# Where ScalarE forms g, what an output of the attention begins with, and which steps convert a second couple of weight blocks

## The chip, the cores and the metric

The kernel runs on one core of one Trainium2 chip. Its metric is the time of one execution on the device, in microseconds (us), the median of the runs shown. TensorE (PE) multiplies; its weight loads are a row of their own (PEld). ScalarE (ACT) and VectorE (DVE) do the elementwise work, GpSimd (POOL) a little more of it, and SyncE (SP) starts nearly all transfers. Each engine takes its instructions in the order in which they stand in its own queue.

## The reference

A decayed attention of 2 batches, 8 heads, 768 positions and 64 columns a head is followed by two feed-forward blocks, all in float32. `S` is the state that goes from block to block.

```python
for b in range(nb):
    qb, kb, vb = (q[:, :, sl], k[:, :, sl], v[:, :, sl])
    intra = np.einsum('bhic,bhjc->bhij', qb, kb) * Dmask[None]
    intra = np.einsum('bhij,bhjd->bhid', intra, vb)
    inter = np.einsum('bhid,bhde->bhie', qb * lam_pow[None], kv_state)
    out[:, :, sl] = intra + inter
    kv_state = lam_block * kv_state + np.einsum('bhsd,bhse->bhde', kb_dec, vb)

x = attn_out                      # 1536 tokens x 512
h = x @ w_in                      # 512 x 2048
g = np.maximum(h, 0.0) ** 2
x = g @ w_out                     # 2048 x 512
gate = 1.0 / (1.0 + np.exp(-(x @ w_gate)))
out = (gate * (x @ w_val)) @ w_out2
```

## The kernel before

**Numbers.** A float32 product is made of three products of rounded halves: a block and an operand are each split into a high part, which ScalarE rounds (`whi`, `gh`, `xh`), and a low part, which VectorE subtracts (`wlo`, `gl`, `xl`). The weights arrive as pairs of 32-bit words of double precision (`raw`). ScalarE makes two words of a block (`scale_words`: `j`, then `r`), VectorE shifts and joins them (`join_words`), the joined block is stored to DRAM for later stages, and `couple_split` makes its high and low parts.

**Couples.** The blocks of the first feed-forward block are converted in couples: the output block of step f together with the input block of step f + 2. There are 17 couples. A couple passes three calls: `couple_act` (four ScalarE instructions, and the next two `raw` loads are queued), `couple_dve` (shift and join on VectorE) and `couple_split` (`whi` on ScalarE, `wlo` on VectorE). I number the couples c0 to c16. Three of them are converted ahead of the loop; the two halves of c0 and c1, one block each, are split there too. Step f splits c(f + 2).

**The stage.** The first 512 tokens go through the first feed-forward block while the rest of the attention is still being computed. `step_1(f)` runs for f = 0 to 15. On PE it gives: `stage_a(f)`, 12 matmuls of 128x512 into one PSUM bank; perhaps the attention work of half 2f; `stage_b(f - 1)`, 12 matmuls of `g` and the output block; perhaps the attention work of half 2f + 1. `SLOTS` says which halves have `scores` (16 matmuls into two banks, later masked by VectorE) or `out` (a state update and an output, 96 matmuls and two banks, which ScalarE copies to `xr`). PSUM has eight banks; four hold the sums of `stage_b` throughout.

**Order.** The program's text is the order on every engine; nothing is rearranged (`tc.manual_schedule`). Before the change, ScalarE in one step does the split of a couple, the four word instructions of the next, and then relu, square and `gh` of the step (lines 525, 526, 538). `MORE = (6, 8, 10)` are the steps that split and convert one couple more.

```python
acc = stage_a(1, f)
run(couple_split())
...
couple_act()
...
gs, ops = split_g(elem(1, f, acc))
```

Stores and some loads stand on an agenda of planned times; they enter SP's queue when the planned clock, which counts matmuls, passes their position. SP waits with a store until its block is joined, and everything behind it in the queue waits too.

**Later stages.** Behind this stage stand a Strassen form of the same feed-forward block for the other 1024 tokens, and the same for the second one. The change doesn't touch their code.

Of the kernel before, what the change touches and what calls it, by code (L numbers as in the profile page):

```python
# [14 lines left out]
TB = 512  # L15
WARM = 14
FILL = (10, 4, 6)
MORE = (6, 8, 10)

PAIRS = ((0, 6), (1, 7), (2, 8), (3, 9), (4, 10), (5, 11))  # L20
LEAD = 2
# [17 lines left out]
def retention_moe_kernel(  # L39
# [24 lines left out]
    nc = tc.nc  # L64
# [15 lines left out]
    def bank():  # L80
        return ps.tile([P, 512], F32, tag="p", name="p")
# [25 lines left out]
    qk_t, kv_t = {}, {}  # L107
# [116 lines left out]
    def couple_split():  # L224
        if not whole_t:
            return []
        keys, w = whole_t.pop(0)
        hi, lo = (several(len(keys), name, F32R) for name in ("whi2", "wlo2"))
        nc.scalar.copy(hi, w)
        for n, key in enumerate(keys):  # L230
            split_t[key] = hi[:, n], lo[:, n]
        return [lambda: nc.vector.tensor_tensor(out=lo, in0=w, in1=hi, op=ALU.subtract)]
# [8 lines left out]
    def run(ops):  # L241
        weave(ops, [])
# [82 lines left out]
    sc_t, qd_t, kd_t, at_t, o_t = {}, {}, {}, {}, {}  # L325
    uv_t, tt_t = [], []

    def pv(t):
        return t.rearrange("a (p b) -> a p b", p=4)

    def half(g):
        return slice(64 * g, 64 * g + 64)

    def held_by(tiles, c, g):


        return tiles[c + 1 if c >= SEQ_CH and g == 0 else c]

    def heads(t):
        return t.rearrange("s (h d) -> s h d", h=H)  # L340
# [64 lines left out]
    def att_out(pair):  # L405


        n = pair[0]
        ov = []
        for s, c in enumerate(pair):  # L410
            v = heads(kv_t[c][:, 1, :])
            at = at_t.pop(c)
            o = pv(bank())
            ov.append(o)
            for p in range(4):
                for r in range(2):
                    nc.tensor.matmul(
                        o[half(r), p, :], lhsT=v[:, 2 * p + r, :],
                        rhs=pv(at[:, r ^ s, :])[:, p, :],
                        start=p == 0, stop=n == 0 and p == 3, skip_group_check=True,  # L420
                    )
        if n > 0:
            for p in range(4):
                for s, c in enumerate(pair):
                    for r in range(2):
                        g = r ^ s
                        nc.tensor.matmul(
                            ov[s][half(r), p, :], lhsT=S[half(g), s, p, :],
                            rhs=pv(held_by(qd_t, c, g))[half(g), p, :],
                            start=False, stop=p == 3, skip_group_check=True,  # L430
                        )
            for c in pair:
                qd_t.pop(c)
        o_t[pair] = ov

    def att_state():
# [682 lines left out]
    def attend(half):  # L1119
        load(LOADS.get(half, ""))  # L1120
        what, k = SLOTS.get(half, (None, 0))
        if what == "scores":
            att_scores(k)
            passed(SCORES)

            def after():
                run(att_mask(k))
                att_keys(k)
                query(k if k < SEQ_CH else k + 1)
                qk_t.pop(k)  # L1130

            return after
        if what == "out":
            pair = PAIRS[k]
            if k < SEQ_CH - 1:
                decayed()
            att_uv(pair)
            att_out(pair)
            for c in pair:
                kv_t.pop(c)  # L1140
            passed(REST)

            def after():
                att_state()
                att_x(pair)

            return after
        return lambda: None

    def step_1(f):  # L1150

        acc = stage_a(1, f)
        run(couple_split())
        while rest:
            rest.pop()()
        attend(2 * f)()
        couple_act()
        if prev:
            stage_b(*prev.pop())
        last = attend(2 * f + 1)  # L1160
        gs, ops = split_g(elem(1, f, acc))
        run(ops)
        run(couple_dve())
        last()
        if f in MORE:
            run(couple_split())
            couple_act()
            run(couple_dve())
        if f + 1 in MORE:
            load_w(2)  # L1170
        prev.append((1, f, gs))
# [25 lines left out]
    with tc.manual_schedule():  # L1197
        load("q6", nc.scalar)
        decays()
        load("q0 q7 v0 v6 w q1 q8 v1 v7 w w w q2 q9")  # L1200
        warm_up(WARM)
        new_xr()
        first, second = PAIRS[:LEAD]
        for c in first:
            att_scores(c)
        warm_up(FILL[0])
        for c in first:
            att_keys(c)
        run([op for c in first for op in att_mask(c)])
        att_uv(first)  # L1210
        for c in (7, 1, 8):
            query(c)
        couple_act()
        for c in second:
            att_scores(c)
        att_out(first)
        att_state()
        x = att_x(first)
        run([op for c in second for op in att_mask(c)])
        run(couple_dve())  # L1220
        warm_up(FILL[1])
        run(x)
        lo = couple_split()
        couple_act()
        run(lo)
        att_out(second)
        run(couple_dve())
        x = att_x(second)
        run(x)
        lo = couple_split()  # L1230
        run(lo)
        couple_act()
        load("v2 v8")
        for c in second:
            att_keys(c)
        decayed()
        att_uv(second)
        run(couple_dve())
        rest.append(att_state)
        for c in (0, 6, 1, 7):  # L1240
            qk_t.pop(c)
        for c in (0, 6, 1, 7):
            kv_t.pop(c)
        clock[0] = 0.0
        flush()


        keys = [(1, i, 0) for i in range(NF1 // 2)]
        prepare_a(keys[0], T1)
        at(T1 - 20.0, lambda: load_a((1, 1, 0)))  # L1250
        combine_x(1, [T1 + d for d in (-25, -22, -19.5, -17, -14, -10, -7, -4, -1, 2, 4)])
        for f in range(NF1):
            step_1(f)
        n_out = 24
        for k in range(3):
            at(T2 - 14.0 + k, lambda: load_w(1))
        for k in range(n_out):
            convert(T2 + 1.0 + k * (T3 - T2 - 4.0) / n_out)
        for f in range(NF1):
            prepare_out(1, f, T2 + 24 * MM * f)  # L1260
        uses = [use for i in range(NF1 // 2) for use in pair_in_1(i)]
        strassen(keys, uses, (None, lambda: close(1)))
        xc.clear()
        new_xr()
        for f in range(2):
            at(T3 - 24.0 + f, lambda f=f: load_units(2, f))
        at(T3 - 14.0, lambda: run(split_w(2, 0)))
        pair_out(1)


        for f in range(2, NF2):
            at(T3 + (36 * (f - 1) - 12) * MM - 8.0, lambda f=f: load_units(2, f))
        for k in range(3 * NF2 - n_out):
            convert(T3 + 2.0 + 3.6 * k)
        for i in range(NF2 // 2):
            sum_out_w(i, T4 - 64.0 + 9.0 * i)
        keys = [(2, i, u) for i in range(NF2 // 2) for u in range(2)]
        prepare_a(keys[0], T4)
        at(T4 - 28.0, lambda: combine_a((2, 0, 1)))
        at(T4 - 20.0, lambda: load_a((2, 0, 1)))  # L1280
        combine_x(2, [T4 - 46.0 + 3.5 * k for k in range(11)])
        for f in range(NF2):
            step_2(f)
        T6 = T5 + 6 * STEP
        by_unit_through_dram(1, T5 - 14.0, T5 - 7.0)
        through_dram(2, T5 - 4.0, T5 + 1.5)
        through_dram(3, T5 + 1.0, T5 + 6.5)
        through_dram(4, T5 + 6.0, T5 + 11.5)
        for n, load, pos in (
            (0, -21.0, -13.0), (1, -12.0, -1.5), (2, -6.0, 4.0),  # L1290
            (3, 1.0, 8.8), (4, 6.0, 13.5), (5, 11.0, 18.3),
        ):
            prepare_w(0, n, n, T5 + load, T5 + pos)
        for n, i, load, pos in (
            (0, 5, -12.5, -5.0), (1, 4, -7.5, -1.0), (2, 3, -3.0, 3.5),
            (3, 0, 1.0, 8.0), (4, 2, 6.0, 12.5), (5, 1, 10.0, 15.5),
        ):
            prepare_w(1, n, i, T6 + load, T6 + pos)
        by_unit_through_dram(2, T6 - 7.0, T6 + 5.0)
        by_unit_through_dram(1, T6, T6 + 10.2)  # L1300
        uses = [use for i in range(NF2 // 2) for use in pair_in_2(i)]
        strassen(keys, uses, (None, lambda: close(2)))
        blocks_out()
        flush()
        assert not agenda and not to_conv and not ready
# [62 lines left out]
```

## Time and profile before

| | us |
|---|---|
| median of 3 runs | 606.05 (604.37 to 606.98) |
| the profiled execution, its own time | 606.55 |
| its span, first to last instruction | 604.8 |
| PE busy in the span | 581.0 (96%) |
| DVE busy | 442.5 (73%) |
| ACT busy | 348.3 (58%) |
| POOL busy | 53.2 (9%) |

The page shows busy time by engine, the span in slices, the queues, the chain that ended last and the costliest groups. Busy PE time includes matmuls at the lower of its two clocks (1.2 against 2.4 GHz), which the windows show as a granted clock of 0.50. A row of the timeline gives the start, the length, engine, line, operation, what is written from what, the number of instructions merged, and in brackets how long the engine had been idle and what ended that.

### The profile page before, as it was taken

The page shows a single profiled execution, that of the slowest core. Times are in us where ns is not written, and L with a number is a line of the kernel's source. Part 1 is how long each engine was busy: PE and PEld are TensorE (multiplying, and loading weights), DVE is VectorE, ACT ScalarE, POOL GpSimd, SP SyncE. Part 2 cuts the span into 40 slices and gives each one's busy share as a digit, 9 for nine tenths or more (in the row PEclk, how much of TensorE's full clock was granted, in tenths as well). Part 3 has the DMA queues.
Part 4 walks back from the last instruction along what each step waited for, and adds up shares of the span by engine and source line. Part 5 has one row for each costly group of instructions (what it writes and reads, how often), then busy time and mean ns, then how long its engine had stood idle before and what let it go on. Part 6 is the DMA issues. An engine that isn't in the chain of part 4 may idle for free.

```text
span 604.8 us, 8511 instructions
## 1 busy us (share of the span) xinstructions
PE 581.0 (96%) x3024; PEld 470.7 (78%) x3024; DVE 442.5 (73%) x632; ACT 348.3 (58%) x548; POOL 53.2 (9%) x51
## 2 busy tenths in 40 slices
PE   8879999888999999999999999999999999999996
PEld 4658777667888888888888888888887888878884
DVE  7765765758688886677674778885578878689964
ACT  3655677576756556666664865534636554475460
POOL 4244240000000000000000000021011101000000
PEclk9979999797999999999999999999999999999999
DMA  8997798532143539999997679994446688488671
GB/s 315 407 411 261 282 310 296 191 106 70 34 157 124 207 104 359 353 412 410 409 407 272 250 253 359 358 303 98 142 111 168 192 249 222 149 321 300 217 279 69
DMA packets 69226, 150.25 MB, mean 248 GB/s; under 512 B 6976, under 2 KB 15168, under 8 KB 69184
## 3 DMA queue, kind: packets, MB, share of 16 engines
q1 hardware_dynamic: 65312, 144.86, 66.8%
q0 software_dynamic: 3360, 3.93, 4.4%
q10 hardware_dynamic: 512, 0.92, 0.5%
q8 instruction: 23, 0.38, 0.3%
q14 instruction: 19, 0.16, 0.1%
HBM read 105.91 MB, written 42.21 MB: 245 GB/s over the span
## 4 chain that ended last, share of the span: by engine, by line
PE 63%; DVE 6%; ACT 5%; DMA 4%; issue 3%; SPq 1%; DVEq 0%; ACTq 0%
PE p L703 27%; PE p L1094 14%; PE p L494 12%; PE p L508 8%; DMA gr<-gs 4%; DVE gq L890 2%; PE p L1023 1%; DVE wq L980 1%; DVE c L717 1%; DVE gs L838 1%; ACT j L154 1%; ACT r L159 1%; DVE j L170 1%; ACT ah L676 1%; DVE al L682 1%
## 5 line engine op out<-in xcount | busy, mean ns | idle before, releaser
L703 PE MATMUL p<-xch,ah 128*128 128x512 f32 x280 | 109.9, 392 | 1.0 <-ACT s L712 0.5
L703 PE MATMUL p<-xcl,ah 128*128 128x512 f32 x280 | 109.0, 389 | 0.0
L703 PE MATMUL p<-xch,al 128*128 128x512 f32 x280 | 109.0, 389 | 0.0
L703 PEld LDWEIGHTS p<-xch,ah 128*128 128x128 f32 x280 | 52.5, 188 | 15.0 <-ACT s L712 3.2
L703 PEld LDWEIGHTS p<-xch,al 128*128 128x128 f32 x280 | 52.6, 188 | 11.0
L712 ACT COPY s<-p 128x512 f32<-128x512 f32 x60 | 35.2, 588 | 45.0 <-PE p L703 44.9
L703 PEld LDWEIGHTS p<-xcl,ah 128*128 128x128 f32 x280 | 52.6, 188 | 10.6
L1023 PE MATMUL p<-gq,wq 128*128 128x512 f32 x252 | 58.3, 391 | 1.6 <-DVE wq L980 1.1
L1023 PEld LDWEIGHTS p<-gq,wq 128*128 128x128 f32 x252 | 47.0, 188 | 12.7 <-DVE wq L980 2.2
L717 DVE TENSOR_TENSOR c<-p,s 128x512 f32<-128x512 f32 x60 | 41.2, 687 | 20.0 <-PE p L703 19.1
L154 ACT ACTIVATE j<-raw 128x512 f32<-128x512 f32 x68 | 45.3, 666 | 9.0 <-DMA raw<-in_w 6.6
L170 DVE CUSTOM_DVE_ANT_0 j<-j,r 128x1024 uint16<-128x1024 uint16 (+1 forms) x53 | 46.4, 875 | 4.9 <-DVE j L165 0.5
L1094 PE MATMUL p<-g2h,whi 128*128 128x512 f32 x128 | 49.8, 389 | 0.0
L1094 PE MATMUL p<-g2l,whi 128*128 128x512 f32 x128 | 49.8, 389 | 0.0
L1094 PE MATMUL p<-g2h,wlo 128*128 128x512 f32 x128 | 49.8, 389 | 0.0
L540 DVE TENSOR_TENSOR gl<-g,gh 128x512 fp32r<-128x512 f32 x28 | 19.8, 708 | 40.5 <-ACT gh L538 40.5
L159 ACT ACTIVATE r<-raw 128x512 int32<-128x512 uint32 x68 | 45.0, 661 | 2.1 <-DMA w<-j 1.9
L494 PE MATMUL p<-xh,whi 128*128 128x512 f32 x160 | 43.7, 395 | 0.1
L508 PE MATMUL p<-gh,whi 128*128 128x512 f32 x112 | 35.5, 434 | 8.1 <-ACT gh L538 8.1
L494 PE MATMUL p<-xh,wlo 128*128 128x512 f32 x160 | 42.9, 390 | 0.0
L494 PE MATMUL p<-xl,whi 128*128 128x512 f32 x160 | 42.8, 389 | 0.0
L651 POOL DMA_DIRECT2D as<-w x6 | 5.6, 926 | 382.0 <-DMA u<-w 306.4
(126 smaller groups left out, 1044.8 us busy)
## 6 DMA issues: line engine op xcount, KB each, us to landing
raw<-in_w SPq DMA_DIRECT2D x68, 512.0 KB, 7.4
w<-j SPq DMA_DIRECT2D x68, 256.0 KB, 6.6
u<-w SPq DMA_DIRECT2D x52, 256.0 KB, 5.4
a<-w SPq DMA_DIRECT2D x20, 512.0 KB, 4.0
g<-g SPq DMA_DIRECT2D x32, 256.0 KB, 4.3
g<-g SPq DMA_DIRECT2D x16, 512.0 KB, 7.7
kv<-in_kv SPq DMA_DIRECT2D x12, 512.0 KB, 7.0
gr<-gs SPq DMA_DIRECT2D x24, 256.0 KB, 6.0
```

The costliest lines, as they stand in the source:

```text
L154: nc.scalar.activation(j, t[:, :, 1].bitcast(F32), AF.Prelu, scale=2.0**-80 if flip else 2.0**-112, alpha=2.0**-32 if flip else 2.0**32,)
L159: nc.scalar.activation(r, low, AF.Copy, scale=2.0**-29)
L170: nc.vector.tensor_tensor(out=j, in0=j, in1=r, op=ALU.add)
L494: nc.tensor.matmul(acc, lhsT=a[:, kk * P : (kk + 1) * P], rhs=b[:, kk, :], start=i == 0, stop=i == 11,)
L508: nc.tensor.matmul(acc[e], lhsT=a[:, e * P : (e + 1) * P], rhs=b, start=first and i == 0, stop=last and i == 2,)
L540: lambda: nc.vector.tensor_tensor(out=gl, in0=src, in1=gh, op=ALU.subtract)
L703: nc.tensor.matmul(acc, lhsT=w[:, col, kk * P : (kk + 1) * P], rhs=x[:, kk, :], start=start and i == 0, stop=stop and i == 5, skip_group_c ...
L712: nc.scalar.copy(s, acc)
L717: nc.vector.tensor_tensor(out=c, in0=acc, in1=s, op=ALU.add)
L890: nc.vector.tensor_tensor(out=block_of(gq[i][1], n), in0=raw.pop(n), in1=block_of(gq[i][0], n), op=ALU.subtract,)
L1023: nc.tensor.matmul(acc[k], lhsT=a[:, wn], rhs=block_of(b, gn), start=first and n == 0, stop=last and n == 3 * len(group) - 1,)
L1094: nc.tensor.matmul(acc[e, t], lhsT=a[:, e * P : (e + 1) * P], rhs=b[:, t, :], start=first and i == 0, stop=last and i == 2,)
```

## The change

In `step_1` the order of the text changes: after `stage_a` come relu, square and `gh`, then the split of a couple, and the word instructions after that. Masks of a half 2f stand ahead of `gl`. In `att_out` the 32 matmuls with the state `S` come first, and open the sums that the 64 with `at` then finish. Ahead of the loop the state of the first pair, its decay and the decayed keys of the second pair stand earlier. Steps 4, 5, 7 and 8, not 6, 8 and 10, convert a second couple, and they no longer split a second one.

```diff
-MORE = (6, 8, 10)
+MORE = (4, 5, 7, 8)
@@ att_out
+        ov = [pv(bank()) for _ in pair]
         if n > 0:
             ...
-                            start=False, stop=p == 3, skip_group_check=True,
+                            start=p == 0, stop=False, skip_group_check=True,
+        for s, c in enumerate(pair):
+            ...
+                        start=n == 0 and p == 0, stop=p == 3, skip_group_check=True,
@@ step_1
         acc = stage_a(1, f)
-        run(couple_split())
         while rest:
             rest.pop()()
-        attend(2 * f)()
-        couple_act()
+        h = 2 * f
+        masks = SLOTS.get(h, ("", 0))[0] == "scores"
+        after = attend(h)
+        gs, ops = split_g(elem(1, f, acc))
+        if masks:
+            after()
+        run(ops)
+        if not masks:
+            after()
+        run(couple_split())
         if prev:
             stage_b(*prev.pop())
-        last = attend(2 * f + 1)
-        gs, ops = split_g(elem(1, f, acc))
-        run(ops)
+        after = attend(h + 1)
+        couple_act()
+        after()
         run(couple_dve())
-        last()
         if f in MORE:
-            run(couple_split())
             couple_act()
             run(couple_dve())
@@ ahead of the loop
         att_uv(first)
+        att_state()
         for c in (7, 1, 8):
             query(c)
+        decayed()
         ...
         att_out(first)
-        att_state()
         ...
+        for c in second:
+            att_keys(c)
         att_out(second)
         ...
-        for c in second:
-            att_keys(c)
-        decayed()
         att_uv(second)
```

ScalarE's queue at steps 0 and 1 before the change; `whi_392` is the split of c2, the next four rows are the words of c3, the three after them belong to step 0:

```order
L229 CAST whi_392<-j_340 128x1024
L154 ACTIVATE j_397<-raw 128x512
L159 ACTIVATE r_398<-raw 128x512
L154 ACTIVATE j_397<-raw 128x512
L159 ACTIVATE r_398<-raw 128x512
L525 ACTIVATE r<-p 128x512
L526 ACTIVATE g<-r 128x512
L538 CAST gh<-g 128x512
```

The same place after the change (its line numbers are two lower here):

```order
L523 ACTIVATE r<-p 128x512
L524 ACTIVATE g<-r 128x512
L536 CAST gh<-g 128x512
L229 CAST whi_401<-j_346 128x1024
L154 ACTIVATE j_405<-raw 128x512
L159 ACTIVATE r_406<-raw 128x512
L154 ACTIVATE j_405<-raw 128x512
L159 ACTIVATE r_406<-raw 128x512
```

The three instructions of g moved from behind five others to ahead of them.

ScalarE's queue before, around step 11: the words of c16, the first split of x (`xch`), the split of c16, then g:

```order
L154 ACTIVATE j_1335<-raw 128x512
L159 ACTIVATE r_1336<-raw 128x512
L154 ACTIVATE j_1335<-raw 128x512
L159 ACTIVATE r_1336<-raw 128x512
L586 CAST xch<-xr 128x1024
L229 CAST whi_1359<-j_1335 128x1024
L525 ACTIVATE r<-p 128x512
L526 ACTIVATE g<-r 128x512
L538 CAST gh<-g 128x512
```

After the change, around the same `xch`:

```order
L229 CAST whi_1317<-j_1046 128x1024
L584 CAST xch<-xr 128x1024
L523 ACTIVATE r<-p 128x512
L524 ACTIVATE g<-r 128x512
L536 CAST gh<-g 128x512
L229 CAST whi_1359<-j_1054 128x1024
L584 CAST xch<-t 128x1024
```

All words are converted by then, c16's in step 9, and one split a step follows g of its step.

## Rows read from the trace of the kernel before

**Rows 1.** Windows: three stretches; engines' busy us, granted clock, DMA share, GB/s.
```profile
0.00:22.30 22.30, 19.38 (x252) 13.08 (x252) 18.08 (x27) 8.95 (x15) 10.90 (x16) 1.00 0.90 344
22.30:159.90 137.60, 123.17 (x853) 98.51 (x854) 89.14 (x98) 90.43 (x141) 24.19 (x17) 0.91 0.67 239
159.90:604.80 444.90, 438.44 (x1921) 359.13 (x1919) 335.27 (x509) 248.87 (x394) 18.11 (x18) 1.00 0.73 247
```

**Rows 2.** Timeline: PE rows of the stage that follow an idle stretch.
```profile
31.73 2.07 PE L508 MATMUL p<-gh,whi 128*128 128x512 f32 x4 [3.65 <-ACT gh L538]
...
44.45 1.91 PE L347 MATMUL p<-qk 64*128 64x128 f32 x14 [2.45 <-DVE at L373]
...
67.43 1.16 PE L347 MATMUL p<-qk 64*128 64x128 f32 x14 [0.58 <-DVE at L373]
...
109.64 2.07 PE L347 MATMUL p<-qk 64*128 64x128 f32 x14 [2.68 <-DVE at L373]
...
138.09 2.08 PE L508 MATMUL p<-gh,whi 128*128 128x512 f32 x4 [4.49 <-ACT gh L538]
```

**Rows 3.** Windows: the four stretches at the lower clock, the first row and the sum.
```profile
31.00:37.80 6.80, 6.07 (x18) 4.46 (x20) 4.95 (x4) 2.34 (x5) 6.80 (x5) 0.50 1.04 411
...
sum 23.30, PE 21.34 PEld 16.87 DVE 18.55 ACT 14.74 POOL 7.48; mean PE 5.33 PEld 4.22 DVE 4.64 ACT 3.69 POOL 1.87
```

**Rows 4.** Timeline, PE: matmuls at the lower clock, then at the higher.
```profile
33.60 1.91 PE L508 MATMUL p<-gh,wlo 128*128 128x512 f32 x4
...
35.30 1.91 PE L508 MATMUL p<-gl,whi 128*128 128x512 f32 x4
...
155.34 1.07 PE L494 MATMUL p<-xh,wlo 128*128 128x512 f32 x4
...
156.24 1.07 PE L494 MATMUL p<-xl,whi 128*128 128x512 f32 x4
```

**Rows 5.** Timeline, steps 0 and 1: PE, VectorE and ScalarE.
```profile
24.29 1.07 PE L494 MATMUL p<-xl,whi 128*128 128x512 f32 x4
...
25.34 1.23 DVE L170 CUSTOM_DVE_ANT_0 j<-j,r 128x2048 uint16<-128x2048 uint16 x1
...
26.60 1.05 ACT L229 CAST whi<-j 128x1024 fp32r<-128x1024 f32 x1 [1.55 <-DVE j L170]
27.01 1.07 PE L494 MATMUL p<-xl,whi 128*128 128x512 f32 x4
27.55 0.67 ACT L154 ACTIVATE j<-raw 128x512 f32<-128x512 f32 x1
...
29.79 0.57 ACT L525 ACTIVATE r<-p 128x512 f32<-128x512 f32 x1
...
31.05 0.62 ACT L538 CAST gh<-g 128x512 fp32r<-128x512 f32 x1
```

**Rows 6.** Timeline, VectorE at steps 4 and 5.
```profile
61.88 0.69 DVE L540 TENSOR_TENSOR gl<-g,gh 128x512 fp32r<-128x512 f32 x1 [4.27 <-ACT gh L538]
62.49 0.69 DVE L165 TENSOR_SCALAR j<-j 128x1024 int32<-128x1024 int32 x1
63.21 1.23 DVE L170 CUSTOM_DVE_ANT_0 j<-j,r 128x2048 uint16<-128x2048 uint16 x1
65.55 1.22 DVE L232 TENSOR_TENSOR wlo<-j,whi 128x1024 fp32r<-128x1024 f32 x1 [1.12 <-ACT whi L229]
66.69 1.28 DVE L373 TENSOR_TENSOR at<-p,D 128x512 f32<-128x512 f32 x2
69.60 0.69 DVE L540 TENSOR_TENSOR gl<-g,gh 128x512 fp32r<-128x512 f32 x1 [1.63 <-ACT gh L538]
```

**Rows 7.** Timeline: VectorE and POOL at the same time, step 1.
```profile
31.75 1.78 POOL L355 TENSOR_TENSOR qd<-qk,L 128x512 f32<-128x512 f32 x1
...
32.31 1.77 DVE L165 TENSOR_SCALAR j<-j 128x1024 int32<-128x1024 int32 x1
...
34.12 1.95 DVE L170 CUSTOM_DVE_ANT_0 j<-j,r 128x2048 uint16<-128x2048 uint16 x1
```

**Rows 8.** Timeline, POOL: the first rows that wait for transfers.
```profile
30.75 1.04 POOL L363 TENSOR_TENSOR kd<-kv,W 128x512 f32<-128x512 f32 x1 [10.78 <-DMA kv<-in_kv]
...
47.32 1.04 POOL L363 TENSOR_TENSOR kd<-kv,W 128x512 f32<-128x512 f32 x1 [9.11 <-DMA kv<-in_kv]
```

More of the change, by code (lines that the diff above doesn't have):

```diff
@@ L408, in att_out @@
         n = pair[0]
[L409 to L421, printed above, removed]
+        ov = [pv(bank()) for _ in pair]
         if n > 0:
@@ L433, in att_out @@
                 qd_t.pop(c)
+        for s, c in enumerate(pair):
+            v = heads(kv_t[c][:, 1, :])
+            at = at_t.pop(c)
+            for p in range(4):
+                for r in range(2):
+                    nc.tensor.matmul(
+                        ov[s][half(r), p, :], lhsT=v[:, 2 * p + r, :],
+                        rhs=pv(at[:, r ^ s, :])[:, p, :],
+                        start=n == 0 and p == 0, stop=p == 3, skip_group_check=True,
+                    )
         o_t[pair] = ov
```

## The prediction

> **What bounds the kernel now.** I read the windows first, cut where the first feed-forward product starts (22.3 us) and where the Strassen blocks start (159.9 us) [rows 1]. Behind 159.9 PE is busy 438.44 of 444.90 us at the full clock: little is to be had there, and the change doesn't touch it. Between the two cuts PE is busy 123.17 of 137.60 us, so it idles 14.4 us, and the granted clock is 0.91 on average. The whole change lies in this stretch and just ahead of it.
>
> The idle time is five pieces that the timeline shows, 13.85 us together [rows 2]. Two end with `gh` (3.65 and 4.49 us), three with the masks (0.58, 2.45 and 2.68 us). Behind each of the four longer ones the granted clock is 0.50; behind the one of 0.58 us it isn't. The windows over those four stretches hold 21.34 us of PE busy time [rows 3]. Four matmuls take 1.70 us from start to start there and 0.90 us at the full clock [rows 4], so this work would have taken 21.34 x 0.90 / 1.70 = 11.3 us: 10.0 us are lost to the clock. PE's work in the stage is thus 123.2 - 10.0 = 113.2 us, 7.1 us a step over 16 steps. Taking all of both away would shorten the kernel by 24.4 us.
>
> Then the cause. At step 0 PE's first input product ends at 24.29 + 1.07 = 25.36 us, but relu starts at 29.79: it stood behind `whi`, which waited for VectorE's join, and four word instructions [rows 5]. In the steps after, the distance from one `gl` to the next is 69.60 - 61.88 = 7.72 us [rows 6]. That is a ring and not PE's pace: ScalarE does split, words, relu, square and `gh`; only then VectorE has `gl`, and behind it shift and join; only then ScalarE may split the next couple. `gl` idled 4.27 us for `gh` there.
>
> **g ahead of the conversions.** No instruction is added or removed, only order. Relu, square and `gh` take 31.05 + 0.62 - 29.79 = 1.88 us [rows 5]. They need only the step's own input product, whose weights were split a step earlier, so they fill the time in which the join runs. The ring that is left is split 0.95 (27.55 - 26.60), words 2.24 (29.79 - 27.55), then shift and join, of which 0.69 + 1.23 less some 0.4 of overlap remain: 4.7 us a step [rows 5, 6]. ScalarE's whole work is 0.95 + 2.24 + 1.88 = 5.1 us, VectorE's 0.69 + 0.69 + 1.23 + 1.22 = 3.8, and 1.28 more for masks [rows 6]. All are below PE's 7.1, so PE becomes the bound.
>
> What is queued behind the new wait: relu now stands at the head of ScalarE's queue until `stage_a` ends, with the split and the words behind it. VectorE waits for those, and PE two steps later. The cover is that lead.
>
> *Step by step at the start.* Relu can start at 25.4, `gh` ends at 27.3, `whi` of c2 (joined at 25.34 + 1.23 = 26.57) at 28.35, and `stage_a(1)` ends at 27.01 + 1.07 = 28.1 [rows 5]. So `stage_b(0)` starts at 28.35, not 31.73, and waits once more for `wlo`: 1.22 behind `whi` against four matmuls in 0.90. I charge 0.6 us. Then c3: words to 30.6, shift and join, split, the four words of c4, and only then relu of step 2. The build gives the second of the two score matmul banks of step 2 the bank which that relu reads, so PE stops there. Shift and join take 1.9 us undisturbed or 3.7 beside POOL (1.77 + 1.95, [rows 7]); relu then ends 0.6 or 2.2 us behind `stage_a(2)`. POOL's keys start at 30.75, when their transfer lands [rows 8], so some disturbance is likely: I take 1.4. The score matmuls of step 7 have the same bank order; there ScalarE is free in time, and the wait is relu alone, 0.6 (0.57 in [rows 5]). In the other steps I find splits and joins ahead of their matmul by 1 us or more. Sum of the new waits: 2.6 us, between 0 and 4.
>
> The piece at 138.09 us goes because relu there stood behind a split of x and behind `whi` of c16, which waited for its join; now g stands first. The two long waits for masks go with the ring: VectorE did `gl`, shift and join ahead of the masks, and all came late.
>
> **State ahead of intra.** The same 32 and 64 matmuls in another order: 0 us. They need `qd` and `S` 2 us earlier and `at` 1 us later; POOL makes `qd` a step ahead. If POOL is late, the price is its longest row here, 1.78 us, for each of four outputs; I keep this in the range.
>
> **Ahead of the loop.** The copy of the state now stands ahead of c0's words and delays them; the four masks ahead of their join on VectorE are the cover. 0 us.
>
> **Other steps for the second couples.** 17 couples as before. An extra couple costs ScalarE 2.24 and VectorE 1.9 us in its step, so ScalarE has 7.3 us in steps 4, 5, 7 and 8, VectorE up to 8.4 in step 4 with two masks. Steps 5 and 8 hold outputs and are longer on PE. The splits left over move to steps 11 to 14: 0.95 and 1.22 us in steps with no words. No term. The loads change place: two `raw` of c6 now stand behind four stores and a query. In this stretch the transfers run at 411 GB/s with a share of 1.04 [rows 3]. Behind the load that lands at 30.75 [rows 8] stand 4.2 MB up to c6, 10.2 us, so c6 lands at 41. ScalarE wants it in step 3 behind g and the split: step 1's product ends at 28.1, step 3's two steps of 7.1 us later at 42.3, and 1.88 + 0.95 make it 45. Cover 4 us.
>
> **The sum.** 606.55 (the profiled execution) - 14.4 (idle) - 10.0 (clock) + 2.6 (new waits) = 584.75. The median of the runs is 0.5 us below this execution: 584.2 us. The stage's first Strassen block would start at 159.9 - 21.8 = 138.
>
> **The rivals.** *POOL in VectorE's way.* For it: [rows 7], a couple's shift and join 1.8 us longer. With masks the ring then has 4.7 + 1.8 + 1.3 = 7.8 us against 7.1: 0.7 in each of eight score steps, 5.6 us, and one fall of the clock at step 2 if the wait reaches the 2.45 us that was enough in [rows 2]; a stretch of 6.8 us at the lower clock costs 6.8 x 0.47 = 3.2. That gives 590 to 593. Against it: PE is two steps ahead of the ring, and out steps are longer.
>
> The Trainium skill, "SBUF — State Buffer", section "Who interferes with whom", speaks for this rival: VectorE and GpSimd share a port pair under an exclusive lock, and the later one fully blocks. The rows agree: the shift came 0.56 us into a POOL row of 1.78, and 1.22 left plus 0.69 of its own is 1.91 against 1.77 measured. By that rule alone two POOL rows a score step, at the mean of 24.19 / 17 = 1.42 us [rows 1], would stand in the ring whole: 4.7 + 1.3 + 2.8 = 8.8 against 7.1, 1.7 in eight steps, and the sum would be near 598.
>
> *Transfers.* If c6 to c8 land late by what is now ahead of c6's loads (1.57 MB at 411 GB/s, 3.8 us), steps 3 to 5 lose up to 11.4 us: 596. Against it: the 4 us of cover.
>
> *Given back later.* The next stage needs blocks from DRAM and the split x; if it were bound by something that doesn't move, the time stays near 606. Against it: PE idles only 6.5 us behind 159.9 [rows 1].
>
> *Slower: the clock.* Small waits at the scores take the place of few long ones. If each of the eight score slots pulled the clock down, 8 x 3.2 = 25.6 us would eat the 21.8: 610. It decides between a gap of 0.58 us, after which the clock stayed, and 2.45, after which it fell [rows 2]; my waits are 0.6 to 1.4, in three places and not eight.
>
> **How the numbers follow.** Forecast 584.2: 0.58. POOL's contention, 588 to 593: 0.26. Transfers, 593 to 602: 0.07. Given back, within 3 us of 606: 0.05. Slower: 0.04. A measurement of this kernel can tell some 0.5%, 3 us. Faster 0.91, same 0.05, slower 0.04. The range runs from 580 (no new wait at all gives 581.6, and attention work may close up a little) to 593, the far end of the contention.
>
> **What would show it.** Right: PE's idle time between the cuts falls from 14.4 to under 4 us, the granted clock there is 1.00 or nearly, relu starts within 0.1 us of the end of `stage_a` in nearly all steps, and the first Strassen block starts near 138 us. The waits that remain are PE for relu or `whi` in steps 1, 2 and 7. Contention: VectorE's shifts near 1.8 us in score steps, and PE waiting for `wlo` or masks. Transfers: ScalarE's words waiting for `raw` loads. The forecast is wrong if a stretch at 0.50 remains in the middle of the stage, or if idle time appears behind the first Strassen block.

## The result, and the profile after

| | before | after |
|---|---|---|
| median of 4 runs, us | 606.51 (604.37 to 607.35) | 586.52 (585.15 to 588.53) |
| the profiled execution, its own time | 606.55 | 585.15 |
| its span | 604.8 | 583.4 |
| PE busy in the span | 581.0 (96%) | 570.9 (98%) |

The ratio of the times is 0.968, with an interval of 0.964 to 0.972: 3.2% faster. The forecast was 584.2 us; 586.5 lies in its range. The two profiled executions differ by 21.4 us where the sum said 21.8. Of the 2.3 us between forecast and median, 0.4 is the sum's; 1.4 is the distance of the profiled execution of after, the fastest of its four runs, from their median; and 0.5 is that of before, which lay above its own and which I carried over.

The windows of the changed kernel, cut where the first feed-forward product starts and where the Strassen blocks start (columns as in [rows 1]):

```profile
0.00:22.10 22.10, 19.29 (x252) 13.12 (x253) 17.10 (x28) 9.19 (x15) 11.19 (x16) 1.00 0.90 343
22.10:137.50 115.40, 113.20 (x856) 90.36 (x853) 88.96 (x96) 87.70 (x138) 28.30 (x17) 1.00 0.76 286
137.50:583.40 445.90, 438.45 (x1921) 359.22 (x1919) 337.69 (x511) 251.34 (x397) 18.11 (x18) 1.00 0.73 246
```

Against [rows 1] the stage takes 115.4 us and not 137.6. PE's busy time there fell from 123.17 to 113.20, its idle time from 14.4 to 2.2, and the granted clock is 1.00 throughout: none of the four stretches at 0.50 is left. ScalarE and VectorE are nearly as busy as before (87.7 and 89.0 us against 90.4 and 89.1), POOL some 4 us more. The part behind the stage is 1.0 us longer (445.9 against 444.9).

PE's rows in the timeline that follow an idle stretch, from the first feed-forward product to 150 us:

```profile
28.09 1.19 PE L506 MATMUL p<-gh,whi 128*128 128x512 f32 x4 [0.24 <-ACT whi L229]
...
36.19 1.16 PE L347 MATMUL p<-qk 64*128 64x128 f32 x14 [0.27 <-ACT r L523]
...
77.94 1.16 PE L347 MATMUL p<-qk 64*128 64x128 f32 x14 [0.27 <-ACT r L523]
...
128.84 1.20 PE L506 MATMUL p<-gh,whi 128*128 128x512 f32 x4 [1.28 <-ACT whi L229]
...
147.98 0.50 PE L701 MATMUL p<-xch,ah 128*128 128x512 f32 x1 [1.71 <-ACT s L710]
```

These answer to [rows 2]. The waits of 3.65 and 4.49 us for `gh` and those of 0.58, 2.45 and 2.68 for the masks are gone. Three small ones stand where the prediction put them (steps 1, 2 and 7). The last two, 1.28 us in step 14 and 1.71 behind the stage, it did not have.

ScalarE's timeline in steps 0 to 2 shows the new order at work:

```profile
25.17 0.60 ACT L523 ACTIVATE r<-p 128x512 f32<-128x512 f32 x1 [0.52 <-PE p L492]
...
26.46 0.62 ACT L536 CAST gh<-g 128x512 fp32r<-128x512 f32 x1
26.99 1.04 ACT L229 CAST whi<-j 128x1024 fp32r<-128x1024 f32 x1
...
35.54 0.60 ACT L523 ACTIVATE r<-p 128x512 f32<-128x512 f32 x1 [0.27 <-PE p L492]
```

At step 0 relu waits for PE now: it starts at 25.17 us, where it started at 29.79 in [rows 5].

### The profile page after: what moved, and what is told of

It reads as the page before. It is cut to its first block, busy times and chain, and to the rows that moved or that the text cites. A ratio compares the mean times of both kernels' runs of the same rounds, so it can differ in the third digit from the quotient of the medians.

```text
span 583.4 us, 8536 instructions
## 1 busy us (share of the span) xinstructions
PE 570.9 (98%) x3024; PEld 462.7 (79%) x3024; DVE 443.8 (76%) x632; ACT 348.2 (60%) x548; POOL 57.6 (10%) x51
## 4 chain that ended last, share of the span: by engine, by line
PE 82%; ACT 6%; DVE 5%; DMA 3%; issue 2%; DVEq 0%; ACTq 0%
PE p L701 27%; PE p L492 17%; PE p L1092 15%; PE p L506 10%; PE p L1021 8%; DMA qk<-in_qk 2%; PE p L427 2%; PE p L347 2%; DVE gq L888 1%; DVE c L715 1%; PE p L415 1%; ACT xch L584 1%; ACT whi L229 1%; DMA gr<-gs 1%; ACT r L523 1%
## 5 line engine op out<-in xcount | busy, mean ns | idle before, releaser
L715 DVE TENSOR_TENSOR c<-p,s 128x512 f32<-128x512 f32 x60 | 41.2, 687 | 20.6 <-PE p L701 19.7
L538 DVE TENSOR_TENSOR gl<-g,gh 128x512 fp32r<-128x512 f32 x28 | 21.1, 753 | 21.1 <-ACT gh L536 21.1
L492 PEld LDWEIGHTS p<-xh,wlo 128*128 128x128 f32 x160 | 30.0, 188 | 6.3
```

The source lines that it names most:

```text
L492: nc.tensor.matmul(acc, lhsT=a[:, kk * P : (kk + 1) * P], rhs=b[:, kk, :], start=i == 0, stop=i == 11,)
L538: lambda: nc.vector.tensor_tensor(out=gl, in0=src, in1=gh, op=ALU.subtract)
L715: nc.vector.tensor_tensor(out=c, in0=acc, in1=s, op=ALU.add)
```

## The experiments

All times are medians; each ratio is against runs of the kernel before that were taken beside it. The kernels ran on more than one chip, so the ratios are the better comparison.

| kernel | us | ratio (95% interval) |
|---|---|---|
| after | 586.5 | 0.968 (0.964 to 0.972) |
| before with the new order in `step_1` alone | 587.2 | 0.969 (0.966 to 0.971) |
| after, second couples in steps 6, 8, 10 | 586.8 | 0.966 (0.964 to 0.969) |
| after, outputs begin with intra | 586.2 | 0.966 (0.963 to 0.968) |
| after with the old order | 617.6 | 1.018 (1.014 to 1.021) |
| after with the old order and steps 6, 8, 10 | 607.4 | 1.001 (1.000 to 1.003) |
| after, split ahead of g | 592.1 | 0.977 (0.973 to 0.981) |
| after, words ahead of g | 591.7 | 0.976 (0.973 to 0.979) |
| after, POOL's products made twice | 595.2 | 0.981 (0.978 to 0.983) |
| before, dummy matmuls in two gaps | 605.9 | 0.999 (0.997 to 1.001) |
| after, two more splits in step 10 | 583.6 | 0.963 (0.960 to 0.966) |
| after, second half of x 2.7 us earlier | **582.1** | 0.960 (0.958 to 0.963) |
| after, both | 582.6 | 0.961 (0.959 to 0.964) |

### Which of the four edits earns the time

The order in `step_1` alone, put into the kernel before (second couples in 6, 8, 10; the old outputs; the old order ahead of the loop):

```diff
         acc = stage_a(1, f)
-        run(couple_split())
...
-        couple_act()
...
+        gs, ops = split_g(elem(1, f, acc))
...
+        run(couple_split())
         if prev:
             stage_b(*prev.pop())
...
-        gs, ops = split_g(elem(1, f, acc))
...
+        couple_act()
...
         if f in MORE:
-            run(couple_split())
```

> The kernel before with the new text of step_1 alone: second couples stay at steps 6, 8, 10 (without their second split), outputs begin with intra, the work ahead of the loop is as before. Theory (the order of g and the conversions earns nearly all of it): 586 to 590 us, PE idle in the stage under 5 us, no stretch at clock 0.50. Rival (the placement of the second couples, or the state first, earns it): 597 us or more.

587.2 us, 0.969. From 22.1 us to its first Strassen block at 138.86 PE idles 3.5 us, at a granted clock of 1.00. The order alone gives the whole gain that can be measured; what the three other edits add is within the measurement (0.969 against 0.968). Taken out of the changed kernel one at a time, two of them show the same:

```diff
-MORE = (4, 5, 7, 8)
+MORE = (6, 8, 10)
```

> The changed kernel with the second couples back at steps 6, 8 and 10. As predicted, placement carries no term: 585 to 588.5 us. Rival (words left for step 10 collide with the first splits of x, or the earlier loads were what kept ScalarE fed): 590 us or more.

586.8 us.

```diff
 att_out
+        (the 64 products with at first)
         (the 32 products with S)
-        (the 64 products with at)
```

> The changed kernel with outputs that begin with intra again. As predicted 0 us: 585 to 588 us. Rival (the masks end so late that the order with at first stops PE in the four outputs): 589 us or more.

586.2 us. Both terms were rightly set to nothing. The order ahead of the loop was not taken out by itself, and neither were two parts of the new `step_1`: the masks ahead of `gl` and the second split that is no longer done. What each of these does alone is not shown.

Then the reverse: the changed kernel with the old order.

```diff
         acc = stage_a(1, f)
+        run(couple_split())
...
+        couple_act()
...
         gs, ops = split_g(elem(1, f, acc))
...
-        run(couple_split())
...
-        couple_act()
         if f in MORE:
+            run(couple_split())
```

> The changed kernel with the old text of step_1: everything else stays changed, so second couples are split and converted at steps 4, 5, 7, 8. Theory: 603 to 609 us, the distance from gl to gl is still 7.7 us in plain steps. Rival: 597 us or less.

A miss: 617.6 us, 1.8% slower than before, where 603 to 609 was expected. The timeline of that kernel between 73 and 103 us, first ScalarE, then PE:

```profile
73.37 1.06 ACT L229 CAST whi<-j 128x1024 fp32r<-128x1024 f32 x1 [2.62 <-DVE j L170]
...
78.37 1.04 ACT L229 CAST whi<-j 128x1024 fp32r<-128x1024 f32 x1 [1.67 <-DVE j L170]
...
81.56 0.57 ACT L523 ACTIVATE r<-p 128x512 f32<-128x512 f32 x1
```

```profile
82.19 2.08 PE L492 MATMUL p<-xh,whi 128*128 128x512 f32 x4 [2.74 <-ACT r L523]
...
96.84 0.79 PE L347 MATMUL p<-qk 64*128 64x128 f32 x2 [3.50 <-ACT r L523]
...
102.28 2.07 PE L347 MATMUL p<-qk 64*128 64x128 f32 x14 [4.65 <-DVE at L373]
```

Between the `gh` at 70.13 and the next relu stand these two splits, each of which waits for its join, and eight word instructions. Relu comes at 81.56 and PE, which needs its bank, stops for 2.74 us, and again for 3.50 one step later. The distance from `gl` to `gl` in plain steps is 7.71 and 7.72 us, as expected. To see whether the second couples do this or the two other edits, the old steps were put back into the same kernel:

```diff
-MORE = (4, 5, 7, 8)
+MORE = (6, 8, 10)
```

> The changed kernel with the old order in step_1 and the old steps (6, 8, 10) of the second couples; so the kernel before with only the outputs that begin with the state and the new order ahead of the loop. Theory (with the old order a second couple lengthens the ring of its step, 4.1 us of ScalarE more ahead of relu, and steps 7 and 8 in a row leave PE no time to recover; the other two edits carry nothing, as with the new order): 604 to 608, and the waits of 2.7, 3.5 and 4.7 us at 82 to 102 us that the kernel with the old order and steps 4, 5, 7, 8 showed are gone. Rival (the state first or the order ahead of the loop does the harm with the old order, since relu's late bank now holds a state product up): 612 to 618, and the waits at 82 to 102 us stay.

607.4 us, ratio 1.001, and of the waits at 82 to 102 us only one of 1.78 us for masks is left: the second couples did it, and the outputs and the order ahead of the loop together carry nothing with the old order either. (A second couple is one split and four words, 0.95 + 2.24 = 3.2 us of ScalarE by [rows 5], not the 4.1 of the expectation.) So the steps of the second couples cost 10 us with the old order, and with the new one no more than can be measured (586.8 against 586.5).

### What has to stand ahead of what

The split ahead of g, the words still last:

```diff
         acc = stage_a(1, f)
...
+        whole = couple_split()
...
-        run(couple_split())
+        run(whole)
```

> The changed kernel with the split of the couple (whi) ahead of g on ScalarE; the words stay last. The ring is then split 0.95, g 1.88, words 2.24, join 1.5: 6.6 us a step, 8.4 with a join beside POOL, against PE's 7.1. Theory: 588 to 595 us, some of the gain goes in the score steps. Rival 1 (only the four word instructions ahead of g did harm): 586 to 587. Rival 2 (anything that waits ahead of g takes the gain back): 600 or more.

592.1 us, in the range of the theory; where it is lost, though, is not where the theory had it, as shown below. The words ahead of g, the split behind it:

```diff
         acc = stage_a(1, f)
...
+        couple_act()
...
         after = attend(h + 1)
-        couple_act()
```

> The changed kernel with the four word instructions ahead of g on ScalarE and the split behind it. The words wait for nothing but their load; the join runs while ScalarE does g and the split. Theory of the ring (what cost the time was that g and gl stood between words and join and the next split): 585 to 589 us. Rival (g must be first, 2.24 us later g costs PE in each of the ten steps with words): 595 us or more.

591.7 us, between the two. The trace says why. PE and ScalarE at the start of the stage, then the windows:

```profile
31.10 1.31 PE L506 MATMUL p<-gh,whi 128*128 128x512 f32 x4 [3.04 <-ACT whi L229]
33.16 2.07 PE L506 MATMUL p<-gh,wlo 128*128 128x512 f32 x4 [0.75 <-DVE wlo L232]
```

```profile
25.94 0.68 ACT L154 ACTIVATE j<-raw 128x512 f32<-128x512 f32 x1 [1.09 <-DMA raw<-in_w]
...
28.21 0.58 ACT L523 ACTIVATE r<-p 128x512 f32<-128x512 f32 x1
```

```profile
31.00:40.00 9.00, 8.15 (x33) 5.89 (x34) 8.89 (x5) 7.21 (x13) 8.36 (x5) 0.62 1.03 408
40.00:141.50 101.50, 100.15 (x793) 80.60 (x792) 74.14 (x84) 71.98 (x112) 18.94 (x12) 1.00 0.69 254
```

At step 0 the words wait 1.09 us for a load, relu comes 3.0 us later than in the changed kernel, and PE loses the difference and the clock (0.62) up to 40 us. From there on PE idles only 1.35 us in 101.5, of which 1.29 is the wait of step 14 that the changed kernel has too. So in the running stage the words may stand on either side of g, as the ring argues; at its start, where PE has no lead yet, they may not. The split ahead of g loses in the same place and more: PE waits 1.26 us for `gh`, 0.66 for `wlo` and then 2.55 for the masks. Steps 3 to 13 lose nothing more, the score steps among them; from step 14 on it is not 4.8 us behind the changed kernel (126.61 against 121.86 at `stage_b` of step 13) but 7.2 (144.67 against 137.50 at the first Strassen block).

```profile
29.13 1.20 PE L506 MATMUL p<-gh,whi 128*128 128x512 f32 x4 [1.26 <-ACT gh L536]
...
30.99 1.20 PE L506 MATMUL p<-gh,wlo 128*128 128x512 f32 x4 [0.66 <-DVE wlo L232]
...
40.10 1.78 PE L347 MATMUL p<-qk 64*128 64x128 f32 x14 [2.55 <-DVE at L373]
```

### The clock by itself

The prediction took 14.4 us of idle time and 10.0 us of lower clock as two terms. Here the kernel before gets 14 and 18 matmuls of a constant tile in bfloat16, whose result nobody reads (3.2 and 4.1 us of PE), ahead of `stage_b` in steps 1 and 11:

```diff
+IDLE = {1: 14, 11: 18}
...
         couple_act()
+        if f in IDLE:
+            warm_up(IDLE[f])
         if prev:
             stage_b(*prev.pop())
```

> The kernel before with matmuls of no use to the result put into two of its idle stretches: 14 ahead of the output product of step 0 (gap of 3.65 us) and 18 ahead of that of step 10 (gap of 4.49 us). They leave the gaps as long as they are and show what the lower clock behind them costs. The sum of the prediction (10.0 us for four stretches, each worth about 3.2): 600 us. If the first stretch lies beside ScalarE's ring and only the second is on PE's path: 603. If neither: 606. If the clock stays low all the same, the granted clock shows it.

605.9 us, ratio 0.999: no gain that can be told from none. Windows over three of the four stretches of [rows 3] in this kernel (its line numbers are one higher):

```profile
31.00:37.80 6.80, 6.21 (x38) 4.91 (x38) 5.01 (x4) 2.32 (x4) 6.80 (x5) 1.00 1.04 408
44.00:48.20 4.20, 3.79 (x18) 3.27 (x19) 3.40 (x5) 4.17 (x7) 0.85 (x1) 0.50 1.05 357
136.80:143.60 6.80, 5.87 (x25) 4.21 (x24) 5.65 (x6) 4.92 (x8) 0.00 (x0) 1.00 0.49 154
```

The dummies did lift the clock in the first and the last of them from 0.50 to 1.00. Behind the first one PE and ScalarE show where the gain went:

```profile
44.41 2.07 PE L348 MATMUL p<-qk 64*128 64x128 f32 x14 [4.01 <-DVE at L374]
```

```profile
36.09 1.06 ACT L230 CAST whi<-j 128x1024 fp32r<-128x1024 f32 x1 [4.48 <-DVE j L171]
...
39.28 0.57 ACT L526 ACTIVATE r<-p 128x512 f32<-128x512 f32 x1
```

PE reaches the scores earlier and waits 4.01 us for the masks, not 2.45, and starts at 44.41 against 44.45 in [rows 2]. ScalarE's ring doesn't know of PE's clock: the split is at 36.09 (36.10 before), the relu behind it at 39.28 (39.30 before). So in the old kernel the lower clock cost nothing in this place, since PE would have waited instead. The second fill misses its gap by one step: the product of step 10, which it stands ahead of, waited for nothing before (127.98 us), and the gap of 4.49 us lies ahead of that of step 11. The fill pushes PE's work into the gap, of which 0.71 us are left. The last stretch did gain: from the product of step 11 to the first Strassen block it is 19.7 us and was 21.8. Half of that is lost again, since that product starts 1.2 us later than before (139.27 against 138.09); 1.1 of these stood there already ahead of the fill (123.46 against 122.40 at the product of step 9). So the full clock was worth nothing in the first stretch and 2.1 us in the last. The two others stayed near 0.50, and what they would give is not shown; the 10.0 us of the four were not to be had by the clock alone in the two that were tried.

### POOL beside VectorE

The strongest rival was VectorE slowed by POOL. POOL's decayed keys and queries are made twice here, all through the kernel:

```diff
+        for _ in range(2):
-        eng.tensor_tensor(
+          eng.tensor_tensor(
...
(the same for the decayed keys)
```

> The changed kernel with each of POOL's decayed keys and queries computed twice into the same tile: POOL's busy time in the stage goes from 28 to about 50 us, nothing else changes. Forecast (PE is two steps ahead of the ring, VectorE's longer joins are covered): 586 to 589.5 us. Rival (contention with POOL sets the remaining waits): 592 us or more, PE waiting for whi, wlo or masks in score steps.

595.2 us, 8.7 more than the changed kernel: by the time alone the rival would hold. By place it does not. PE rows that follow an idle stretch (lines two higher than in the changed kernel):

```profile
21.94 1.97 PE L417 MATMUL p<-qd,S 64*64 64x128 f32 x26 [2.35 <-POOL qd L356]
...
28.15 0.69 PE L401 MATMUL p<-kv,kd 128*64 128x64 f32 x16 [1.18 <-POOL kd L365]
...
37.56 1.20 PE L508 MATMUL p<-gh,wlo 128*128 128x512 f32 x4 [1.61 <-DVE wlo L232]
...
44.80 1.16 PE L347 MATMUL p<-qk 64*128 64x128 f32 x14 [0.68 <-ACT r L525]
...
86.57 1.16 PE L347 MATMUL p<-qk 64*128 64x128 f32 x14 [0.27 <-ACT r L525]
```

Ahead of the stage PE waits for POOL itself: the first `stage_b` starts at 34.74 us, 6.65 later than at 28.09. At the scores of step 2 the delay is 8.61 (44.80 - 36.19), at those of step 7 8.63 (86.57 - 77.94), at the first Strassen block 9.26. So a doubled POOL costs steps 1 and 2 some 2.0 us, the steps from there to 7 nothing, and the rest 0.6. In the stage `wlo` then takes 1625 ns in the mean and not 1442: VectorE is slowed further, and PE's lead covers nearly all of it except at the start.

### The two waits that were not predicted

ScalarE's rows of the changed kernel around steps 11 to 14, then two of VectorE's:

```profile
111.17 0.60 ACT L523 ACTIVATE r<-p 128x512 f32<-128x512 f32 x1 [3.18 <-PE p L492]
...
117.61 1.05 ACT L584 CAST xch<-t 128x1024 fp32r<-128x1024 f32 x1 [3.56 <-DVE t L600]
118.56 0.59 ACT L523 ACTIVATE r<-p 128x512 f32<-128x512 f32 x1
...
124.98 1.05 ACT L584 CAST xch<-t 128x1024 fp32r<-128x1024 f32 x1 [3.56 <-DVE t L600]
125.94 0.58 ACT L523 ACTIVATE r<-p 128x512 f32<-128x512 f32 x1
...
127.75 1.04 ACT L229 CAST whi<-j 128x1024 fp32r<-128x1024 f32 x1
```

```profile
113.12 0.69 DVE L538 TENSOR_TENSOR gl<-g,gh 128x512 fp32r<-128x512 f32 x1 [4.82 <-ACT gh L536]
...
116.35 1.22 DVE L600 TENSOR_TENSOR t<-xr 128x1024 f32<-128x1024 f32 x1
```

It is the old ring with another member. `xch`, the split of a piece of x for the Strassen blocks, stands ahead of relu and waits for VectorE's `t`; `t` stands behind `gl`, `wlo` and `xcl`; `gl` waits for `gh`, which follows relu. One round takes 118.56 - 111.17 = 7.39 us, the next 7.38. PE needs 116.42 - 110.98 = 5.44 for a step without attention work. Two rounds lose 3.9 us, PE's lead is used up, and `stage_b` of step 14 waits 1.28.

Three kernels, each the changed one with one edit or both. Two more splits ahead of that place:

```diff
         run(couple_split())
+        if f == 10:
+            run(couple_split())
+            run(couple_split())
         if prev:
             stage_b(*prev.pop())
```

> The changed kernel with two more splits of finished couples in step 10, so that steps 11 to 14 split one couple each and no second one. Theory (the wait of 1.28 us of PE for whi at step 13 comes from a full ScalarE and VectorE behind step 11, where five extra splits of 0.95 and 1.22 us stand beside the splits of x): that wait goes and the time falls by 1 to 2.5 us against the changed kernel, 584 to 585.5, first Strassen block at 136.2 to 136.5 us. Rival (the wait is made by xch standing ahead of relu and waiting for VectorE's t, 3.56 us twice, not by the splits): the row stays, within 0.5 us of the changed kernel, 586 to 587.

The second half of the split of x earlier:

```diff
-        combine_x(1, [T1 + d for d in (-25, -22, -19.5, ...)])
+        combine_x(1, [T1 + d - 2.7 for d in (-25, -22, -19.5, ...)])
```

> The changed kernel with the eleven pieces of the second half of the split of x planned 2.7 us earlier. Theory (the first Strassen blocks wait 1.71 us for sums s that ScalarE forms late, because the pieces of x stand late in its queue now that the stage ends 22 us earlier): the wait of 1.71 us goes, and the time falls by 1 to 2 us, 584.5 to 585.5. Rival (the pieces then stand ahead of relu in more steps of the first stage, where xch waits for VectorE): a wait of 1 to 3 us appears at steps 11 to 14 in exchange, 586 to 589.

> Both edits: two more splits in step 10, and the second half of the split of x 2.7 us earlier. Theory (the two waits have separate causes): both gains add, 2 to 3 us less than the changed kernel, 583.5 to 585. Rival (both waits come from one full ring of ScalarE and VectorE behind step 10): the sum is no more than the better of the two alone, 585 to 587.

583.6, 582.1 and 582.6 us. With more splits ahead the two waits shrink to 0.44 and 1.11 us. The earlier pieces of x gain 4.4 us by the medians and 2.8 by the profiled executions (582.31 against 585.15), more than was expected, since they take away both waits: 1.28, and 1.71 less the 0.47 that are left, make 2.5. All three times lie below the ranges of their theories. The profiled execution of the changed kernel is the fastest of its four, so the gains by the medians may be too large. In the kernel with the earlier pieces ScalarE finds `t` ready, and PE's only wait worth naming is 0.47 us:

```profile
114.00 1.05 ACT L584 CAST xch<-t 128x1024 fp32r<-128x1024 f32 x1
116.67 0.60 ACT L523 ACTIVATE r<-p 128x512 f32<-128x512 f32 x1 [1.62 <-PE p L492]
```

```profile
144.30 0.50 PE L701 MATMUL p<-xch,ah 128*128 128x512 f32 x1 [0.47 <-ACT s L710]
```

Relu waits for PE again, a step takes 122.11 - 116.67 = 5.44 us there, and the first Strassen block starts at 135.51, 2.0 us earlier. The gains don't add (582.6 for both). That fits the rival for the third kernel, that both waits come from one full ring, though its range of 585 to 587 was missed: more splits ahead, which leave the pieces of x where they are, shorten the second wait too. The extra splits treat a part of the load, the earlier pieces the member that closes the ring. The kernel with the earlier pieces is the best of all: 4.0% under the one before, and its interval (0.958 to 0.963) ends below that of the changed kernel (0.964 to 0.972).

## Why the prediction was right, point by point

**The cause.** Right, and shown: the order in `step_1` alone brings the gain, and taking it back loses it. What VectorE's `gl` waits for in the stage shows the ring come apart (operations by line and form: count, busy us and mean ns, then idle us ahead of it and for whom), before and after:

```profile
L540 DVE TENSOR_TENSOR gl<-g,gh 128x512 fp32r<-128x512 f32 x16 | 11.5, 720 | 32.3 <-ACT gh L538 32.3
```

```profile
L538 DVE TENSOR_TENSOR gl<-g,gh 128x512 fp32r<-128x512 f32 x15 | 12.1, 805 | 12.2 <-ACT gh L536 12.2
```

One sign was put too strongly: relu was to start with the end of `stage_a` in nearly all steps. It does so within 0.1 us in 8 of 16; in the others it comes 0.4 to 3.9 us later. PE's lead covers that except at the worst, step 13 (125.94 against 120.95 + 1.07): the split for which PE waits 1.28 us stands behind that relu.

**The sum.** Idle time was to fall by 14.4 and return by 2.6; it fell by 14.4 - 2.2 = 12.2. The work was to fall by 10.0 to 113.2; it is 113.20. That it agrees to the tenth is luck: ends of matmuls are modelled and some of a wait counts as busy, and the kernel with the earlier pieces of x, which does the same work, has 112.56 in its stage. The first Strassen block was forecast for 138 and stands at 137.50. That the clock was added as a term of its own was sound only because the ring went too; in the old kernel the full clock gave nothing in one stretch and 2.1 us in another, and no gain in the whole time that can be told from none.

**The new waits.** The sum was near, its parts were not all right.

| place | charged, us | measured |
|---|---|---|
| step 1, `whi` and `wlo` | 0.6 | 0.24 + (29.35 - 28.09 - 0.90) = 0.60 |
| step 2, relu's bank | 1.4 | (37.28 - 35.43) - (32.49 - 31.39) = 0.75 |
| step 7, the same | 0.6 | (79.02 - 77.18) - (74.23 - 73.14) = 0.75 |
| step 14, `whi` | 0 | 1.28 |
| first Strassen blocks, `s` | 0 | 1.71 |

The figures for steps 2 and 7 are distances from start to start: two score banks with the wait between them, less two banks' worth without one (16 matmuls in 1.10 us). The last two figures are idle times, so the column doesn't add up to the 2.2 us of the stage. Step 2 was charged with a shift and a join slowed by POOL; they ran at 0.69 and 1.23 us, since both began ahead of POOL's row at 30.79. The step that failed is "The splits left over move to steps 11 to 14 ... No term": I counted their own time and not what they do to the splits of x behind them. With it fell the sentence that in the other steps splits come 1 us or more ahead of their matmul: in step 14 PE waits 1.28 us for one. And "given back later" happened on a small scale: the stage ends 22 us earlier, ScalarE isn't done with the pieces of x, and 1.0 of those us are lost behind it.

**The rivals.** POOL's contention was there: `wlo` took 2.32 us beside POOL in step 1. It cost the changed kernel's PE nothing that a row shows, and even doubled no more than 2.6 us in the stage. The sum near 598, by the rule of the Trainium skill ("SBUF — State Buffer", section "Who interferes with whom") with every POOL row a full place in the ring, fell: the rows are delayed as it says, but PE's lead and the waits of relu for PE leave room for it. (That sum, like the one of 590 to 593, counted eight score steps; eight halves have scores, in seven steps, as step 4 has two.) Transfers: no word instruction of the stage waits for a load; one waited 3.17 us for PE (at 83.89), and PE lost nothing. Slower by the clock: the small waits of 0.24 to 1.71 us left it at 1.00 throughout. With the old order and the new steps of the second couples that rival's time (610) was even passed, at 617.6, but by the ring and not by small waits.

## What to carry to other kernels

When two engines release each other in turn, write down the round as a chain of queue entries, the waits included, and compare its length with the pace of the engine that should be the bound; then put the member that the next round needs at the head of its queue, and the work that can wait behind it. An engine's lower clock or slower rows beside such a ring may be worth little of their own until the ring is shorter than that engine's work. After the change look for the next ring with the same eyes: here it was the split of x, found in the idle time of two queues, and it was worth another 3 to 4 us.

## What the runs showed of the hardware

The length of a gap alone didn't decide PE's clock. In the kernel with the old order and steps 6, 8, 10, a gap of 2.54 us was followed by the full clock (granted 1.00 from 111.8 to 116.5 us):

```profile
111.80 1.16 PE L347 MATMUL p<-qk 64*128 64x128 f32 x14 [2.54 <-DVE at L373]
```

In [rows 2] one of 2.45 us was followed by the lower one. With the split ahead of g, waits of 1.23 and 0.66 us in step 14, with four matmuls between them, were followed by the lower one too (granted 0.55 from 135.7 to 139.0 us), where the wait of 1.28 us in the changed kernel left it at 1.00. What else decides was not tried.

How much POOL delays VectorE depends on the operands. POOL and VectorE of the changed kernel, step 1 to 2:

```profile
32.67 1.74 POOL L355 TENSOR_TENSOR qd<-qk,L 128x512 f32<-128x512 f32 x1
34.38 2.02 POOL L363 TENSOR_TENSOR kd<-kv,W 128x512 f32<-128x512 f32 x1
```

```profile
33.18 2.32 DVE L232 TENSOR_TENSOR wlo<-j,whi 128x1024 fp32r<-128x1024 f32 x1
35.42 1.27 DVE L373 TENSOR_TENSOR at<-p,D 128x512 f32<-128x512 f32 x2
```

```profile
30.79 1.92 POOL L363 TENSOR_TENSOR kd<-kv,W 128x512 f32<-128x512 f32 x1 [11.28 <-DMA kv<-in_kv]
```

```profile
30.58 1.23 DVE L170 CUSTOM_DVE_ANT_0 j<-j,r 128x2048 uint16<-128x2048 uint16 x1
```

`wlo`, with both inputs in SBUF, starts 1.23 us ahead of the end of POOL's row (34.41) and takes 2.32 us, near 1.23 + its own 1.22. The two masks, which read one input from PSUM, take 1.27 us beside POOL's rows, as alone (1.28 in [rows 6]). The join of step 1 begins 0.21 us ahead of POOL's row and takes 1.23 us, as alone; there POOL's row is the one that is delayed, 1.92 us against 1.04 for the same row in [rows 8]. The Trainium skill, "SBUF — State Buffer", section "Who interferes with whom", says just this: a VectorE instruction with at most one SBUF input, outside its two-port modes, doesn't contend with GpSimd, and one with two SBUF inputs does, with a GpSimd instruction that reads SBUF. I had not used that half of the rule: it takes the masks out of the rival's sum.
